# One core, attention, experts and a dense pair: the numerator of a rational function nested from PSUM, tokens scaled by a diagonal product, and eight pieces of w_out made float32 earlier

## The chip, the cores and the metric

The kernel runs on one core of one Trainium2 chip. The metric is the device time of one execution in microseconds (us), the median of several runs. The engines go by the names of the profile: PE is the matrix engine (PEld its weight loads), DVE the vector engine, ACT the scalar engine, POOL the GpSimd engine and SP the queue that starts most DMAs. L12 is line 12 of the kernel before, unless the text says that it is of the changed kernel.

## The reference

Three stages follow each other. The third is the one that most of this is about.

```python
x = attention(q_l, k_l, v_l, q_g, k_g, v_g)     # 2304 tokens of 512
e = argmax(x @ w_gate)                          # one of 8 experts for each token
y = c * (relu(x @ w1[e]) @ w2[e])               # c: one factor for each token
h = y @ w_in                                    # 512 -> 2048
P = a[0] + a[1]*h + a[2]*h**2 + a[3]*h**3
Q = 1.0 + abs(b[0])*abs(h) + abs(b[1])*h**2
out = (P / (Q + 1e-6)) @ w_out                  # 2048 -> 512
```

[...] For precision every product runs on numbers that are split into two parts of a reduced float32 (high and low), and three of the four part products are summed.

## The kernel before

**Attention** (up to some 160 us into the span) ends with the gate of the last batch, a chain of small operations written as a generator that is advanced a few steps at a time between the matmuls of expert 0. Its last part writes the lists of tokens: L624 on DVE, a transpose on PE (L627) and a copy on DVE (L629).

**The experts** follow one another, 0 to 7. The tokens of an expert are gathered by an indirect DMA of POOL in blocks of 128 (L755), multiplied by their factor c (`scale`: L767 on ACT or L769 on POOL or DVE, 128x512), transposed by four PE instructions against an identity (`prep`, L780) and split (L760 on ACT, L761 on DVE). `wide` then runs eight pieces of 12 matmuls into a `ph` tile (L870; two such tiles), with relu and split on ACT and DVE (L875, L876), and two pieces later 12 matmuls into `acc` (L882). Between them, in 32 slots for one expert, a plan hands out other work by a letter: `s` splits a piece of the next expert's weights (L682 on ACT, then L686 on POOL or DVE), `c` is one of three DVE operations that make a piece of `w_in` or `w_out` float32 (`conv_step`: L703, L706, L709, all into the one tile `f`), `g` gathers, `x` scales and `p` transposes. After the third operation SP writes the piece to DRAM (L727) and loads the next 64-bit piece (L729), so the next L703 waits for that write. SP also loads the next expert's weights (L672), in the same order as the program.

**The dense pair** (`moe2`, from 458 us) takes the tokens in five chunks of 4, 3, 4, 3 and 3 tiles of 128 (`CH`). A chunk has 16 steps, one for each 128 columns of h: PE computes h two steps ahead (L1090, 12 matmuls of 512 or 384 columns) and multiplies by a piece of `w_out` three steps behind (L1138, 12 or 9 matmuls of 512). Between the two lies the rational function of one step, over three engines:

- ACT: sq = h*h (L1099), q = |b0 h| (L1100), u = a3 h + a2 (L1102);
- DVE: q = b1 sq + q (L1101). POOL: u = u sq (L1103);
- of the step before, the split of the quotient: gh on ACT (L1108), gl on POOL in the first 16 steps and on DVE after (L1109);
- ACT: r0 = exp(-ln(q + 1 + 1e-6)) in two instructions (L1111, L1112);
- DVE: u = a1 h + u (L1116), then a step of Newton (L1119, L1122) and u = (u + a0) r (L1126).

Through the first 16 steps (chunk 0) `w_out` is made ready, a piece a step, by a generator that is advanced once after each of L1116, L1119 and L1122: three DVE operations make a piece float32 (L703, L706, L709 again, into `io`), then ACT and POOL split it (L1170, L1171). Two of the sixteen pieces come as float32 from DRAM, since they were made during the experts (`NPRE`); for them those three advances do nothing. Where the next chunk's tokens are split (L1045 on ACT, L1046 on DVE), a step has two more operations. At the end of a chunk the results are copied out of PSUM (L1147) and scattered by POOL (L1149, L1150). Each engine works through its instructions in program order.

Of the kernel before, what the change touches and what calls it, by code (L numbers as in the profile page):

```python
# [42 lines left out]
NX = 4  # L43
SA, S0, S1 = "v", "a", "p"

# [9 lines left out]

NPRE, NCONV = 2, 9
WLO = lambda nc, f: nc.gpsimd
PLANW = plan(32, s=range(0, 31, 2), c=range(2, 29, 3), g=(6, 9, 20, 24), x=(1, 2, 16, 18), p=(5, 8, 19, 22))
PLANW7 = plan(32, s=range(2, 18, 2))
# [23 lines left out]
AHEAD = 2  # L83
GL = lambda nc, s: nc.gpsimd if GL0 <= s < 16 else nc.vector
GL0 = 0
CH = (4, 3, 4, 3, 3)
ER = {"sq": 1, "q": 2, "u": 2, "r0": 1}
CQ = lambda nc: nc.sync
# [13 lines left out]
class Build:  # L102
# [26 lines left out]
    def attn_consts(self, ap, inner):  # L129
# [362 lines left out]
    def gate(self, b, xT=None, woven=0):  # L492
# [126 lines left out]
        if last:  # L619
            self.places(self.idx, self.tab)  # L620
            self.counts()
            yield

            nc.vector.tensor_tensor(out=self.wrap, in0=self.tab, in1=self.wrap, op=ALU.subtract)  # L624
            yield
            pt = ps_m.tile([128, 512], F32, tag="xps", name="lgT")[:, 0:128]
            nc.tensor.transpose(pt, self.wrap[:, 0:128], self.ident)  # L627
            yield
            nc.vector.tensor_copy(self.idxT, pt)  # L629
        elif b == B - 2:  # L630
# [25 lines left out]
    def load_raw(self, e, pc):  # L656

        nc, t = self.nc, self.t
        if e > 9 or pc >= (16 - NPRE // 2 if e == 9 else 8):
            return  # L660
        r = self.raws[e, pc] = self.raw[pc % 4]
        if e == 9 and pc >= NPRE // 2:
            RQ(nc).dma_start(out=r.bitcast(I64), in_=t["w64"][16 + NPRE // 2 + pc])
            return
        if e < E:
            if pc < 4:
                src = t["w1"][e][:, pc, :].rearrange("p (a f) -> p a f", a=2)
            else:
                src = t["w2"][e][:, 2 * pc - 8:2 * pc - 6, :]
        else:  # L670
            src = self.wf[16 * (e - 8) + 2 * pc:16 * (e - 8) + 2 * pc + 2].rearrange("a p f -> p a f")
        RQ(nc).dma_start(out=r.rearrange("p (a f) -> p a f", a=2), in_=src)  # L672
# [47 lines left out]
    def conv_step(self, k):  # L720

        q, n = divmod(k, 3)
        if not 0 <= q < 16 + NPRE:
            return
        self.conv_op(self.r64[q % 2], self.f32[q % NF], n)
        if n == 2:
            CQ(self.nc).dma_start(out=self.wf[q], in_=self.f32[q % NF].bitcast(F32))  # L727
            if q + 2 < 16 + NPRE:
                CQ(self.nc).dma_start(out=self.r64[q % 2], in_=self.t["w64"][q + 2])  # L729

# [52 lines left out]

    def experts(self, st, first, gate):
# [184 lines left out]
        def woven():  # L969
# [87 lines left out]
    def moe2(self):  # L1057
        nc, tc, out = self.nc, self.tc, self.t["out"]
        with ExitStack() as st:
# [257 lines left out]
```

## Time and profile before

| | before |
|---|---|
| median of 3 runs | 904.21 us (902.74 to 906.9) |
| the profiled execution | 907.55 us, its span 905.9 us |
| busy in the span | PE 812.4 us (90%), DVE 681.7 (75%), ACT 520.9 (58%), POOL 411.4 (45%) |
| the chain that ended last | DVE 31% of the span, ACT 9%, issue 6%, POOL 2%, PE 1% |

A busy PE is not a PE at its peak. In the timelines a line has the start in us from the span's start, the busy time in us, the engine, the line and operation, and output and inputs; what ended an idle time stands in brackets.

### The profile page before, as it was taken

How to read it: one execution, taken by the hardware profiler on the slowest of the kernel's cores; microseconds unless marked ns; L12 is line 12 of the kernel's file. 1: busy time of each engine (PE TensorE's matmuls, PEld its weight loads, DVE VectorE, ACT ScalarE, POOL GpSimd, SP SyncE). 2: the span in 40 equal slices, each digit the busy share in tenths (PEclk: the TensorE clock that was granted, in tenths of full speed). 3: DMA queues.
4: the chain of work that ended last, by engine and by line, in shares of the span. 5: the costliest groups of instructions: out<-in, count | busy, mean ns of one | idle time of the engine just before them, and what ended most of it. 6: DMA issues, size and time to landing. Idle time of an engine off the chain costs nothing. (4 is left out here: it accounts for less than half of the span.)

```text
span 905.9 us, 17033 instructions
## 1 busy us (share of the span) xinstructions
PE 812.4 (90%) x6093; PEld 675.6 (75%) x6093; DVE 681.7 (75%) x1428; ACT 520.9 (58%) x1195; POOL 411.4 (45%) x443
## 2 busy tenths in 40 slices
PE   7999998888998998899996987789999998998994
PEld 4767765776988898887974755577778887987882
DVE  4678777752836775661479999989989997998895
ACT  3667666343544554442465555567776766777664
POOL 3445546452747776650465555542242234223322
PEclk8999999998999999999997999999999999999998
DMA  8798872561738788760433223011000001000000
GB/s 289 238 318 267 271 248 77 161 223 46 262 118 284 258 275 274 237 227 26 154 118 93 82 70 94 1 46 36 13 35 12 13 1 47 1 1 12 24 1 36
DMA packets 48626, 112.94 MB, mean 125 GB/s; under 512 B 8763, under 2 KB 20204, under 8 KB 46466
## 3 DMA queue, kind: packets, MB, share of 16 engines
q1 hardware_dynamic: 39938, 97.18, 33.1%
q0 software_dynamic: 4288, 10.06, 3.6%
q10 hardware_dynamic: 4288, 4.29, 1.5%
q8 instruction: 59, 0.97, 0.5%
q14 instruction: 53, 0.43, 0.1%
HBM read 96.47 MB, written 18.98 MB: 127 GB/s over the span
## 5 line engine op out<-in xcount | busy, mean ns | idle before, releaser
L1103 POOL TENSOR_TENSOR u<-u,sq 128x384 f32<-128x384 f32 (+1 forms) x80 | 104.4, 1305 | 201.0 <-ACT u L1102 198.8
L1138 PE MATMUL acc<-slot,gh 128*128 128x512 f32 x544 | 175.9, 402 | 14.9 <-ACT raw L1147 5.6
L1090 PE MATMUL ph<-x2c,slot 128*128 128x512 f32 (+1 forms) x576 | 136.0, 387 | 15.8 <-DVE u L1116 13.7
L686 POOL TENSOR_TENSOR slot<-raw,slot 128x512 fp32r<-128x512 f32 x80 | 111.5, 1398 | 69.5 <-ACT slot L682 64.1
L1090 PEld LDWEIGHTS ph<-x2c,slot 128*128 128x128 f32 x576 | 107.1, 192 | 40.5 <-DVE u L1116 19.1
L1138 PEld LDWEIGHTS acc<-slot,gh 128*128 128x128 f32 x544 | 102.6, 191 | 41.7 <-POOL slot L1171 7.5
L1138 PE MATMUL acc<-slot,gl 128*128 128x512 f32 x272 | 109.0, 401 | 1.0 <-DVE gl L1109 1.0
L882 PE MATMUL acc<-hT,slot 128*128 128x256 f32 (+1 forms) x768 | 105.1, 288 | 0.2 <-DVE hT L876 0.2
L882 PEld LDWEIGHTS acc<-hT,slot 128*128 128x128 f32 x768 | 98.4, 192 | 0.4 <-DVE hT L876 0.4
L1101 DVE SCALAR_TENSOR_TENSOR q<-sq,cab,q 128x384 f32<-128x384 f32 (+1 forms) x80 | 95.9, 1199 | 2.2 <-ACT q L1100 1.8
L682 ACT CAST slot<-raw 128x512 fp32r<-128x512 f32 x144 | 84.1, 618 | 13.6 <-DVE yt L888 5.6
L1108 ACT CAST gh<-u 128x384 fp32r<-128x384 f32 (+1 forms) x80 | 44.6, 558 | 78.4 <-DVE u L1126 57.1
L1090 PE MATMUL ph<-xa,slot 128*128 128x384 f32 x384 | 75.8, 346 | 10.7 <-DVE u L1116 10.7
L1090 PEld LDWEIGHTS ph<-xa,slot 128*128 128x128 f32 x384 | 68.3, 192 | 18.9 <-DVE u L1116 17.4
L1111 ACT ACTIVATE r<-q,cab 128x384 f32<-128x384 f32 (+1 forms) x80 | 52.9, 661 | 50.3 <-DVE q L1101 49.7
L312 POOL TENSOR_SCALAR pr<-ex,r 128x128 f32<-128x128 f32 x128 | 46.6, 376 | 67.4 <-PE sc L258 20.8
L686 DVE TENSOR_TENSOR slot<-raw,slot 128x512 fp32r<-128x512 f32 x64 | 60.8, 953 | 10.1 <-ACT slot L682 8.7
L1122 DVE SCALAR_TENSOR_TENSOR r<-q,r 128x384 f32<-128x384 f32 (+1 forms) x80 | 64.9, 811 | 2.3
L1126 DVE SCALAR_TENSOR_TENSOR u<-u,cab,r 128x384 f32<-128x384 f32 (+1 forms) x80 | 64.3, 803 | 2.3
L1116 DVE SCALAR_TENSOR_TENSOR u<-ph,cab,u 128x384 f32<-128x384 f32 (+1 forms) x80 | 52.8, 660 | 13.2 <-POOL u L1103 13.2
L1138 PEld LDWEIGHTS acc<-slot,gl 128*128 128x128 f32 x272 | 51.5, 189 | 14.7 <-DVE gl L1109 2.6
L294 ACT ACTIVATE ex<-sm,mx 128x128 f32<-128x128 f32 x128 | 50.2, 395 | 16.8 <-POOL pr L312 8.5
(202 smaller groups left out, 1548.4 us busy)
## 6 DMA issues: line engine op xcount, KB each, us to landing
raw<-in_w_dram SPq DMA_DIRECT2D x78, 512.0 KB
vw<-in_vw_dram SPq DMA_DIRECT2D x16, 1024.0 KB
r<-in_w_dram SPq DMA_DIRECT2D x18, 512.0 KB
kw<-in_kw_dram SPq DMA_DIRECT2D x16, 384.0 KB
wf<-f SPq DMA_DIRECT2D x18, 256.0 KB
raw<-wf SPq DMA_DIRECT2D x9, 512.0 KB
qt<-in_qT_dram SPq DMA_DIRECT2D x32, 128.0 KB
xbuf<-xrow SPq DMA_DIRECT2D x8, 512.0 KB
```

The source lines that it names most:

```text
L294: nc.scalar.activation(ex[:, h], src[:, h], AF.Exp, bias=mx[:, h:h + 1], scale=-1.0, accum_out=ssum[:, h:h + 1])
L682: nc.scalar.copy(hi, r)
L686: eng.tensor_tensor(out=lo[:, c], in0=r[:, c], in1=hi[:, c].bitcast(F32), op=ALU.subtract)
L882: nc.tensor.matmul(acc[m][:, :n], lhsT=W[:, b, 8 + f, 128 * m:128 * m + 128], rhs=hT[f % nh][:, a, :n], start=(f == 0 and i == 0), stop=(f ...
L1090: nc.tensor.matmul(ph[:, :w], lhsT=l[a], rhs=r[b], start=(k == 0 and i == 0), stop=(k == 3 and i == 2))
L1101: nc.vector.scalar_tensor_tensor(out=q, in0=sq, scalar=b1, in1=q, op0=ALU.mult, op1=ALU.add)
L1103: nc.gpsimd.tensor_tensor(out=u, in0=u, in1=sq, op=ALU.mult)
L1111: nc.scalar.activation(r0, q, AF.Ln, bias=eps1)
L1116: nc.vector.scalar_tensor_tensor(out=u, in0=h, scalar=a1, in1=u, op0=ALU.mult, op1=ALU.add)
L1122: nc.vector.scalar_tensor_tensor(out=r0, in0=q, scalar=2.0, in1=r0, op0=ALU.subtract, op1=ALU.mult, reverse0=True)
L1126: nc.vector.scalar_tensor_tensor(out=u, in0=u, scalar=a0, in1=r0, op0=ALU.add, op1=ALU.mult)
L1138: nc.tensor.matmul(accs[i], lhsT=l[a], rhs=Wo[:, b, f, :], start=(f == 0 and j == 0), stop=(f == 15 and j == 2))
```

## The change

Four things are changed.

1. **Numerator and denominator of the rational function.** ACT computes ab = |h|, u = a3 h + a2 and q = b1 ab + b0, the last from SBUF. POOL computes q = q ab. DVE computes u = h u and u = (u + a1) h, both with h read from PSUM. gl is on DVE in all steps. The number of instructions of ACT in a step stays at six, that of DVE is six in every step, that of POOL one.
2. **Tokens are scaled by a diagonal.** `scale` writes c times the identity (128x128) into `dg`, by ACT where POOL did it; `prep` multiplies the raw tokens by it on PE in place of the transpose.
3. **Pieces of w_out.** Every other piece, eight in place of two, is made float32 during the experts: 12 operations an expert in place of 9. In `w_out` a piece of 64 bits and one of float32 alternate.
4. **The last lists** of the gate move into a generator that is advanced between the matmuls of expert 0; the copy goes to ACT.

```diff
-SA, S0, S1 = "v", "a", "p"
+SA, S0, S1 = "v", "a", "a"
-NPRE, NCONV = 2, 9
+NPRE, NCONV = 8, 12
+LOADS = [l for j in range(NPRE // 2) for l in ((4 * j, 4 * j + 2), (4 * j + 1,), (4 * j + 3,))]
-PLANW = plan(32, s=range(0, 31, 2), c=range(2, 29, 3), g=(6, 9, 20, 24), x=(1, 2, 16, 18), p=(5, 8, 19, 22))
+PLANW = plan(32, s=range(0, 31, 2), c=(2, 3, 7, 8, 12, 13, 17, 18, 21, 23, 25, 27), g=(6, 9, 20, 24), x=(1, 2, 16, 18), p=(5, 8, 19, 22))
-GL = lambda nc, s: nc.gpsimd if GL0 <= s < 16 else nc.vector
+GL = lambda nc, s: nc.vector
-            yield
-            nc.vector.tensor_tensor(out=self.wrap, in0=self.tab, in1=self.wrap, op=ALU.subtract)
-            yield
-            pt = ps_m.tile([128, 512], F32, tag="xps", name="lgT")[:, 0:128]
-            nc.tensor.transpose(pt, self.wrap[:, 0:128], self.ident)
-            yield
-            nc.vector.tensor_copy(self.idxT, pt)
+    def lists(self):
+        self.nc.vector.tensor_tensor(out=self.wrap, in0=self.tab, in1=self.wrap, op=ALU.subtract)
+        yield
+        yield
+        pt = self.ps_m.tile([128, 512], F32, tag="xps", name="lgT")[:, 0:128]
+        self.nc.tensor.transpose(pt, self.wrap[:, 0:128], self.ident)
+        yield
+        self.nc.scalar.copy(self.idxT, pt)
...
-        xg = self.xgs[j % len(self.xgs)][:rows]
-        x, c = xg[:, :DM], xg[:, DM:]
+        d, c = self.dg[j % len(self.dg)][:rows, :rows], self.xgs[j % len(self.xgs)][:rows, DM:]
         if eng == "a":
-            self.nc.scalar.activation(x, x, AF.Copy, scale=c)
+            self.nc.scalar.activation(d, self.ident[:rows, :rows], AF.Copy, scale=c)
...
-            nc.tensor.transpose(pt[:, c], xg[:rows, 128 * c:128 * c + 128], self.ident[:rows, :rows])
+            nc.tensor.matmul(pt[:, c], lhsT=xg[:rows, 128 * c:128 * c + 128], rhs=self.dg[j % len(self.dg)][:rows, :rows],
+                             start=True, stop=True)
...
+        self.dg = [r[:, 0:128] for r in hr]
...
-                    nc.scalar.activation(sq, h, AF.Square)
-                    nc.scalar.activation(q, h, AF.Abs, scale=b0)
-                    nc.vector.scalar_tensor_tensor(out=q, in0=sq, scalar=b1, in1=q, op0=ALU.mult, op1=ALU.add)
+                    nc.scalar.activation(ab, h, AF.Abs)
                     nc.scalar.activation(u, h, AF.Identity, scale=a3, bias=a2)
-                    nc.gpsimd.tensor_tensor(out=u, in0=u, in1=sq, op=ALU.mult)
+                    nc.scalar.activation(q, ab, AF.Identity, scale=b1, bias=b0)
+                    nc.gpsimd.tensor_tensor(out=q, in0=q, in1=ab, op=ALU.mult)
+                    nc.vector.tensor_tensor(out=u, in0=h, in1=u, op=ALU.mult)
+                    nc.vector.scalar_tensor_tensor(out=u, in0=u, scalar=a1, in1=h, op0=ALU.add, op1=ALU.mult)
+                    for _ in range(SPN(s)[0]):
+                        next(sp, None)
...
-                    nc.vector.scalar_tensor_tensor(out=u, in0=h, scalar=a1, in1=u, op0=ALU.mult, op1=ALU.add)
-                    for _ in range(SPN(s)[0]):
-                        next(sp, None)
                     nc.vector.scalar_tensor_tensor(out=q, in0=q, scalar=1.0 + 1e-6, in1=r0, op0=ALU.add, op1=ALU.mult)
```

Three places show how the order of the instructions moves.

DVE in chunk 0 of the dense pair, before: one step, with a piece of `w_out` being made float32 (`io`).

```order
L1101 SCALAR_TENSOR_TENSOR q_8580<-sq_8578,cab,q_8580 128x512
L1116 SCALAR_TENSOR_TENSOR u_8582<-ph_8913,cab,u_8582 128x512
L709 SCALAR_TENSOR_TENSOR io<-raw_77,io 128x512
L1119 SCALAR_TENSOR_TENSOR q_8580<-q_8580,r_8583 128x512
L703 TENSOR_SCALAR io<-raw_74 128x512
L1122 SCALAR_TENSOR_TENSOR r_8583<-q_8580,r_8583 128x512
L706 SCALAR_TENSOR_TENSOR io<-raw_74,io 128x512
L1126 SCALAR_TENSOR_TENSOR u_8582<-u_8582,cab,r_8583 128x512
```

And in the change: a step that ends a piece (L714 of the changed kernel is its third operation) and the next, which has none of the three until its L1128.

```order
L1112 TENSOR_TENSOR u_8613<-ph_8984,u_8613 128x512
L1113 SCALAR_TENSOR_TENSOR u_8613<-u_8613,cab,ph_8984 128x512
L714 SCALAR_TENSOR_TENSOR io<-raw_77,io 128x512
L1121 TENSOR_TENSOR gl_8607<-u_8614,gh_8604 128x512
L1128 SCALAR_TENSOR_TENSOR q_8611<-q_8611,r_8615 128x512
L1131 SCALAR_TENSOR_TENSOR r_8615<-q_8611,r_8615 128x512
L1135 SCALAR_TENSOR_TENSOR u_8613<-u_8613,cab,r_8615 128x512
L1200 SCALAR_TENSOR_TENSOR od_8617<-order,od_8617 128x17
L1112 TENSOR_TENSOR u_8614<-ph_9027,u_8614 128x512
L1113 SCALAR_TENSOR_TENSOR u_8614<-u_8614,cab,ph_9027 128x512
L1121 TENSOR_TENSOR gl_8608<-u_8613,gh_8605 128x512
L1128 SCALAR_TENSOR_TENSOR q_8612<-q_8612,r_8615 128x512
```

L1101 is gone, L1112 and L1113 stand where L1101 and L1116 stood, gl (L1121) has come to DVE, and the two conversions between L1128 and L1135 stand in every second step only.

ACT in a step of 512 columns after chunk 0 (chunk 2), before:

```order
L1099 ACTIVATE sq_8578<-ph_10205 128x512
L1100 ACTIVATE q_8580<-ph_10205,cab 128x512
L1102 ACTIVATE u_8582<-ph_10205,cab 128x512
L1108 CAST gh_8573<-u_8581 128x512
L1111 ACTIVATE r_8583<-q_8580,cab 128x512
L1112 ACTIVATE r_8583<-r_8583 128x512
```

And in the change:

```order
L1108 ACTIVATE ab_8610<-ph_10210 128x512
L1109 ACTIVATE u_8614<-ph_10210,cab 128x512
L1110 ACTIVATE q_8612<-ab_8610,cab 128x512
L1120 CAST gh_8605<-u_8613 128x512
L1123 ACTIVATE r_8615<-q_8612,cab 128x512
L1124 ACTIVATE r_8615<-r_8615 128x512
```

The last of the three ACT operations ahead of gh now makes q, which goes through POOL before the logarithm (L1123 of the changed kernel) can start.

DVE in an even expert, before:

```order
L876 SCALAR_TENSOR_TENSOR hT_3362<-ph,hT_3362 128x256
L686 TENSOR_TENSOR slot_3337<-raw_74,slot_3337 128x512
L703 TENSOR_SCALAR f_0_3786<-r_1_3785 128x512
L876 SCALAR_TENSOR_TENSOR hT_3363<-ph,hT_3363 128x256
L706 SCALAR_TENSOR_TENSOR f_0_3786<-r_1_3785,f_0_3786 128x512
L761 TENSOR_TENSOR xa<-pt,xa 128x4x128
L686 TENSOR_TENSOR slot_3337<-raw_75,slot_3337 128x512
L876 SCALAR_TENSOR_TENSOR hT_3364<-ph,hT_3364 128x256
```

And in the change:

```order
L884 SCALAR_TENSOR_TENSOR hT_3364<-ph,hT_3364 128x256
L691 TENSOR_TENSOR slot_3339<-raw_74,slot_3339 128x512
L708 TENSOR_SCALAR f_0_3788<-r_0_3786 128x512
L711 SCALAR_TENSOR_TENSOR f_0_3788<-r_0_3786,f_0_3788 128x512
L884 SCALAR_TENSOR_TENSOR hT_3365<-ph,hT_3365 128x256
L767 TENSOR_TENSOR xa<-pt,xa 128x4x128
L691 TENSOR_TENSOR slot_3339<-raw_75,slot_3339 128x512
L714 SCALAR_TENSOR_TENSOR f_0_3788<-r_0_3786,f_0_3788 128x512
L884 SCALAR_TENSOR_TENSOR hT_3366<-ph,hT_3366 128x256
L708 TENSOR_SCALAR f_0_3788<-r_1_3787 128x512
L767 TENSOR_TENSOR xa<-pt,xa 128x4x128
```

The first operation on the next piece (L708) follows the third on the piece before (L714) with one L884 between them, where a wait for the write of `f` can now stand; two more operations on pieces of w_out lie among the expert's own.

## Rows read from the trace of the kernel before

**Rows 1.** Windows: us, busy us of each engine, clock, DMA share; experts, then chunk 0.

```profile
285.70:401.30 115.60, 102.56 (x834) 100.79 (x834) 78.21 (x124) 57.60 (x120) 81.19 (x64) 0.97 0.79 259
458.00:586.00 128.00, 103.01 (x426) 79.32 (x424) 124.55 (x141) 75.57 (x125) 69.23 (x51) 0.96 0.25 76
```

**Rows 2.** Chain that ended last: start us, us, what; chunk 0, then chunk 3.

```profile
547.09 1.70 DVE r L1122
577.74 1.68 DVE r L1122
773.58 1.39 DVE q L1101
831.74 1.38 DVE q L1101
```

**Rows 3.** Timeline of PE (start us, us, engine line op, tiles); four tiles, then three.

```profile
719.58 2.96 PE L1090 MATMUL ph<-x2c,slot 128*128 128x512 f32 x12
725.17 2.96 PE L1090 MATMUL ph<-x2c,slot 128*128 128x512 f32 x12
735.66 2.26 PE L1090 MATMUL ph<-xa,slot 128*128 128x384 f32 x12
737.76 0.63 PE L1138 MATMUL acc<-slot,gh 128*128 128x512 f32 x2
```

**Rows 4.** Timeline of DVE and POOL in chunk 0, steps of 512 columns.

```profile
478.32 0.68 DVE L1122 SCALAR_TENSOR_TENSOR r<-q,r 128x512 f32<-128x512 f32 x1
478.57 1.58 POOL L1103 TENSOR_TENSOR u<-u,sq 128x512 f32<-128x512 f32 x1 [0.45 <-ACT u L1102]
478.93 1.77 DVE L706 SCALAR_TENSOR_TENSOR io<-raw,io 128x512 int32<-128x512 int32 x1
481.95 0.74 DVE L1116 SCALAR_TENSOR_TENSOR u<-ph,cab,u 128x512 f32<-128x512 f32 x1
482.09 1.27 POOL L1109 TENSOR_TENSOR gl<-u,gh 128x512 fp32r<-128x512 f32 x1 [1.94 <-ACT gh L1108]
```

**Rows 5.** Timeline of one step of chunk 3, 384 columns, ACT, DVE and POOL.

```profile
811.48 0.62 ACT L1111 ACTIVATE r<-q,cab 128x384 f32<-128x384 f32 x1 [0.72 <-DVE q L1101]
812.13 0.53 ACT L1112 ACTIVATE r<-r 128x384 f32<-128x384 f32 x1
812.56 0.47 ACT L1099 ACTIVATE sq<-ph 128x384 f32<-128x384 f32 x1
813.39 0.67 ACT L1102 ACTIVATE u<-ph,cab 128x384 f32<-128x384 f32 x1
813.87 0.62 DVE L1126 SCALAR_TENSOR_TENSOR u<-u,cab,r 128x384 f32<-128x384 f32 x1
814.14 1.22 POOL L1103 TENSOR_TENSOR u<-u,sq 128x384 f32<-128x384 f32 x1 [3.11 <-ACT u L1102]
815.81 0.62 ACT L1111 ACTIVATE r<-q,cab 128x384 f32<-128x384 f32 x1 [0.72 <-DVE q L1101]
```

**Rows 6.** Timeline of DVE where chunk 1 begins, in brackets its idle time and releaser.

```profile
601.37 0.62 DVE L1116 SCALAR_TENSOR_TENSOR u<-ph,cab,u 128x384 f32<-128x384 f32 x1 [2.74 <-POOL u L1103]
```

**Rows 7.** Groups by line: tiles, shapes, count | busy us, mean ns | idle and releasers.

```profile
L780 PE MATMUL pt<-ident,xg 128*128 128x128 f32 (+1 forms) x132 | 20.8, 284 | 14.2 <-POOL xg L769 10.1 <-DVE xa L761 3.4 <-PE sc L258 0.6
L627 PE MATMUL lgT<-ident,wrap 128*128 128x128 f32 x1 | 0.5, 475 | 2.4 <-DVE wrap L624 2.4
L258 PE MATMUL sc<-kw,qt 128*64 128x128 f32 x512 | 47.6, 308 | 1.6 <-DVE mx L264 0.8 <-DMA kw<-in_kw_dram 0.8
```

**Rows 8.** Timeline of SP and DVE in an expert, then groups by line.

```profile
354.39 0.33 SPq L727 DMA_DIRECT2D wf<-f  x1
358.48 0.43 DVE L703 TENSOR_SCALAR f<-r 128x512 int32<-128x512 int32 x1 [2.41 <-DMA wf<-f]
...
L703 DVE TENSOR_SCALAR f<-r 128x512 int32<-128x512 int32 x18 | 11.6, 643 | 16.7 <-DMA wf<-f 10.7 <-issue 4.9 <-DVE x2c L761 1.0
L882 PE MATMUL acc<-hT,slot 128*128 128x256 f32 (+1 forms) x768 | 105.1, 288 | 0.2 <-DVE hT L876 0.2
```

More of the change, by code (lines that the diff above doesn't have):

```diff
@@ L83 @@
 AHEAD = 2
-GL = lambda nc, s: nc.gpsimd if GL0 <= s < 16 else nc.vector
-GL0 = 0
+GL = lambda nc, s: nc.vector
 CH = (4, 3, 4, 3, 3)
-ER = {"sq": 1, "q": 2, "u": 2, "r0": 1}
+ER = {"ab": 1, "q": 2, "u": 2, "r0": 1}
 CQ = lambda nc: nc.sync
@@ L142, in attn_consts @@
         self.wg, self.tok = wg.rearrange("p (c e) -> p c e", c=4), tok
+        self.dg = [ap.tile([128, 128], F32, name=f"dg{n}") for n in range(2)]
         self.xTg = inner.tile([128, NP, 128], F32, name="xTg")
@@ L658, in load_raw @@
         nc, t = self.nc, self.t
-        if e > 9 or pc >= (16 - NPRE // 2 if e == 9 else 8):
+        if e > 9 or pc >= (len(LOADS) if e == 9 else 8):
             return
         r = self.raws[e, pc] = self.raw[pc % 4]
-        if e == 9 and pc >= NPRE // 2:
-            RQ(nc).dma_start(out=r.bitcast(I64), in_=t["w64"][16 + NPRE // 2 + pc])
+        if e == 9 and len(LOADS[pc]) == 1:
+            RQ(nc).dma_start(out=r.bitcast(I64), in_=t["w64"][16 + LOADS[pc][0]])
             return
@@ L670, in load_raw @@
         else:
-            src = self.wf[16 * (e - 8) + 2 * pc:16 * (e - 8) + 2 * pc + 2].rearrange("a p f -> p a f")
+            q = 2 * pc if e == 8 else 16 + LOADS[pc][0] // 2
+            src = self.wf[q:q + 2].rearrange("a p f -> p a f")
         RQ(nc).dma_start(out=r.rearrange("p (a f) -> p a f", a=2), in_=src)
@@ L728, in conv_step @@
             if q + 2 < 16 + NPRE:
-                CQ(self.nc).dma_start(out=self.r64[q % 2], in_=self.t["w64"][q + 2])
+                n = q + 2 if q < 14 else 16 + 2 * (q - 14)
+                CQ(self.nc).dma_start(out=self.r64[q % 2], in_=self.t["w64"][n])
     def counts(self):
@@ L761, in split_t, with scale @@
         self.nc.vector.tensor_tensor(out=lo, in0=pt, in1=hi.bitcast(F32), op=ALU.subtract)
-    def scale(self, j, rows=128, eng="p"):
-        xg = self.xgs[j % len(self.xgs)][:rows]
-        x, c = xg[:, :DM], xg[:, DM:]
+    def scale(self, j, rows=128, eng="a"):
+        d, c = self.dg[j % len(self.dg)][:rows, :rows], self.xgs[j % len(self.xgs)][:rows, DM:]
         if eng == "a":
-            self.nc.scalar.activation(x, x, AF.Copy, scale=c)
+            self.nc.scalar.activation(d, self.ident[:rows, :rows], AF.Copy, scale=c)
         else:
             (self.nc.gpsimd if eng == "p" else self.nc.vector).tensor_scalar(
-                out=x, in0=x, scalar1=c, scalar2=1.0, op0=ALU.mult, op1=ALU.mult)
+                out=d, in0=self.ident[:rows, :rows], scalar1=c, scalar2=1.0, op0=ALU.mult, op1=ALU.mult)
     def prep(self, j, x, ps, at=None, rows=128, scale=True, skip=0):
@@ L983, in woven @@
                 pass
-            yield from todo(0, PLAN0, 1, blocks(1, (0, 1)) + blocks(0, (2, 3)),
-                            blocks(1, (0, 1)) + blocks(0, (2, 3)) + blocks(2, (0, 1)) + blocks(1, (2, 3)))
+            yield from weave(todo(0, PLAN0, 1, blocks(1, (0, 1)) + blocks(0, (2, 3)),
+                                  blocks(1, (0, 1)) + blocks(0, (2, 3)) + blocks(2, (0, 1)) + blocks(1, (2, 3))),
+                             self.lists())
         acc = [ps_a.tile([128, 512], F32, tag=f"acc{m}", name=f"acc{m}") for m in range(4)]
@@ L1097, in elem @@
                     h = hs.pop(s)[:, :w]
-                    sq, q, u, r0 = (et[t_][s % len(et[t_])][:, :w] for t_ in ("sq", "q", "u", "r0"))
-                    nc.scalar.activation(sq, h, AF.Square)
-                    nc.scalar.activation(q, h, AF.Abs, scale=b0)
-                    nc.vector.scalar_tensor_tensor(out=q, in0=sq, scalar=b1, in1=q, op0=ALU.mult, op1=ALU.add)
+                    ab, q, u, r0 = (et[t_][s % len(et[t_])][:, :w] for t_ in ("ab", "q", "u", "r0"))
+                    nc.scalar.activation(ab, h, AF.Abs)
                     nc.scalar.activation(u, h, AF.Identity, scale=a3, bias=a2)
-                    nc.gpsimd.tensor_tensor(out=u, in0=u, in1=sq, op=ALU.mult)
+                    nc.scalar.activation(q, ab, AF.Identity, scale=b1, bias=b0)
[4 more added lines that the diff above has]
+                        next(sp, None)
                 if 1 <= s <= n_steps:
@@ L1158, in w_out @@
             def w_out():
+                where = {f: (pc, i) for pc, l in enumerate(LOADS) for i, f in enumerate(l)}
+                done, nxt = set(), 4
                 for f in range(16):
-                    pc = f // 2 if f < NPRE else f - NPRE // 2
-                    if f < NPRE:
-                        w = self.raws[9, pc][:, 512 * (f % 2):512 * (f % 2) + 512]
+                    pc, i = where[f]
+                    if len(LOADS[pc]) == 2:
+                        w = self.raws[9, pc][:, 512 * i:512 * i + 512]
                         for k in range(3):
@@ L1171, in w_out @@
                     WLO(nc, f).tensor_tensor(out=Wo[:, 1, f, :], in0=w, in1=Wo[:, 0, f, :].bitcast(F32), op=ALU.subtract)
-                    if f >= NPRE or f % 2:
-                        self.load_raw(9, pc + 4)
+                    done.add(f)
+                    while nxt < len(LOADS) and done.issuperset(LOADS[nxt - 4]):
+                        self.load_raw(9, nxt)
+                        nxt += 1
             sp = w_out()
```

## The prediction, as put on record before the change ran

> **What bounds the kernel now.** I read the windows first, to see which engine is full in which stage, then the chain that ended last for the pace of a step, then timelines for single steps, and last the groups by line and their waits for the experts. In chunk 0 of the dense pair DVE is busy for 124.55 of 128.00 us and PE for 103.01 [rows 1]: DVE sets the pace there. Four steps lie between the two L1122 of the chain, (577.74 - 547.09) / 4 = 7.66 us a step [rows 2]. PE alone would need 5.59 us for the 24 matmuls of such a step (725.17 - 719.58) [rows 3], that is 0.233 each. After chunk 0 there is no conversion of `w_out`, and the two meet. A step of 512 columns runs at PE's 5.59. A step of 384 columns needs 2.10 us for L1090 (737.76 - 735.66) and 9 x 0.233 = 2.10 for L1138, 4.20 in all [rows 3], and takes 4.33 from one logarithm to the next (815.81 - 811.48) [rows 5]; 13 steps of chunk 3, three or four of them with a split of the next tokens, average (831.74 - 773.58) / 13 = 4.47 [rows 2]. Here the loop of ACT and DVE sets the pace, 0.13 to 0.27 behind PE. In the experts PE is busy for 102.56 of 115.60 us, DVE for 78.21, and DMA for 0.79 [rows 1]: PE is the bound, with holes.
>
> **What two engines do to each other.** L1122 took 0.68 us with POOL free; L706, of the same size and kind, took 1.77 when a POOL operation had started 0.36 before it [rows 4]: 1.09 lost to one meeting. L1116, which reads h from PSUM, took 0.74 with POOL's L1109 in the middle of it [rows 4]. The other way round, L1126 had started first, kept its 0.62, and POOL's L1103 ended 0.87 after it [rows 5]. So a DVE operation on SBUF alone and a POOL operation exclude each other, first come first, and one with PSUM on one side is free. The changed numerator has both its operations on PSUM.
>
> **The step of 384 columns, walked.** E is the end of Exp, 812.66. ACT starts its next operation 0.10 before E, the next after 0.37, and the third 0.56 after that, which is u's 0.67 less the same overlap [rows 5]. So ab starts at -0.10, u at 0.27 and q at 0.83. q reads SBUF with two scalars, which no row shows; between Exp's 0.53 and u's 0.67 I take 0.65. POOL's product is ready at about 1.55. DVE's last operation holds from 1.21 to 1.83 as before, so the product ends at 1.83 + 0.87 = 2.70. The two new DVE operations (0.6 each, as L1116 has 0.62 at this size [rows 6]) lie beside it. The logarithm starts 0.08 later, Exp 0.65 after that, and E comes again at 2.70 + 0.08 + 0.65 + 0.53 = 3.96. That is under PE's 4.20, so PE takes over: 13 steps in each of chunks 1 and 3 go from 4.47 to 4.25 (splits do not all hide), and 13 in chunk 4 from 4.33 to 4.20. That makes -5.7 and -1.7, **-7.5**. Its ends are -9.5 (4.20 everywhere) and +8 (4.53, if the loop is 0.57 longer than walked). Steps of 512 columns after chunk 0 are PE's before and after: 0.
>
> **Chunk 0.** A step that converts loses one of three meetings with POOL (-1.09) and gets gl back (+0.68, as L1122): -0.41. Against that the logarithm now waits for POOL, which also has the split of `w_out`; I give the 0.41 back and take 0 for these eight. Six further steps lose their conversion: 0.43 (L703 [rows 8]) and twice 0.68, 1.79 us, of which 0.5 is spent on waiting for the product. I take -1.3 x 6 = **-8**. The other two had none before. Ends: all fourteen at PE's pace, 14 x (5.59 - 7.66) = -29; or nothing, 0.
>
> **Boundaries and ends.** Where chunk 1 begins, DVE waited 2.74 us for POOL's product behind the scatters [rows 6], with the logarithm long done. Now the logarithm and Exp, 1.18 us, come after that product, where L1116's 0.62 [rows 6] came: +0.56 at four boundaries, **+2.2**. Filling the pipe and draining it are each about one us longer by ACT's third operation and POOL's: **+2**. Ends 0 and +8 for both.
>
> **Tokens.** PE sat idle for 10.1 us in front of transposes because POOL's scaling was late [rows 7]; it stands in POOL's queue between splits of weights. A diagonal of 128 columns on ACT costs less than the 0.53 of an Exp of 384 [rows 5], and nothing on POOL. ACT now waits for gathers itself, with L875 behind it, and `dg` shares its memory with `hr`, so once or twice it waits for a store. I take **-8**; ends -10 and 0. The product itself: a plain float32 matmul of 128 columns has a mean of 308 ns, the transpose 284 [rows 7]. Over 132 that is 3 us at the most; the longer one reads its weights with a stride, so I take 0. The Trainium skill, FP8 and Floating Point Precision, TensorE Precision Notes, says that true float32 takes four passes through the array. By that four times a quarter of 0.233 would be paid for each, an estimate of up to 23 us more in the sum; the 308 beside the 284 speaks against it, and it is the fourth rival below.
>
> **The lists.** PE waited 2.4 us for L624 [rows 7]; now matmuls of expert 0 stand there: **-2**, ends -2.4 and 0.
>
> **More conversion in the experts.** Eighteen DVE operations, 6 x 1.79 = 11 us, lie on an engine with 37 us free in 115 [rows 1]. Six writes and six 64-bit loads join SP's queue, in front of weight loads that are four pieces ahead; DMA has a fifth of its time left; in chunk 0 SP has 12 loads of `w_out` in place of 15. The new wait: L703 waits for the write of `f`, which was issued at 354.39 and let L703 start at 358.48, 4.1 us [rows 8]. With two pairs of pieces an expert now back to back, DVE stands still up to 12 x 4.1 = 49 us, and L876 and the splits queue behind it. Before, such waits made 10.7 us and PE waited for L876 for 0.2 [rows 8]: two tiles of `ph` cover a late L876. I take **+2**; ends 0 and +18 (a third of the 49 uncovered).
>
> **Sum.** -7.5 - 8 + 2.2 + 2 - 8 - 2 + 2 = -19.3. The profiled execution took 907.55, 3.3 above the median of the runs, and would take 888.3; from the median 904.21 it is 884.9. I predict **885 us**.
>
> **Rivals.**
> - *Chunk 0 falls further.* With POOL down to two operations a step, DVE may win the meetings, and converting steps go from 7.66 to 6.5, the others from 6.36 to PE's 5.6. For: only luck of order holds the 0.41 back. Against: both POOL operations start while DVE has SBUF work. 885 - 8 x 1.16 - 8 x 0.76 = 870.
> - *The stalls in the experts show.* For: two waits of 4 us an expert are new; against: the 0.2 above. It decides when DVE is later than the two `ph` tiles cover. 885 - 2 + 18 = 901.
> - *Slower: the new operations on h exclude POOL after all.* Then the product gets its turn only at 3.03, after both, ends at 3.90, and E comes again at 5.16 in place of 4.33 over some 42 steps: 885 + 7.5 + 35 = 927. It decides when the product ends later than 3.07 after E. For: they read SBUF too. Against: L1116 and L1109 above.
> - *The diagonal product is a full float32 one.* Place: PE in the experts, the bound there. If it takes 128 columns as long as L1090 takes 512, 0.233, and not the quarter of it, 0.058, it adds 132 x 0.175 = 23: 885 + 23 = 908. For: it has no row of its own. Against: 308 beside 284. This is also what the page named above would make of it.
> - *It does not do what it says:* float32 pieces come late from DRAM, the chunk waits for its loads as long as it converted. For: loads now wait for two pieces to be done; against: two steps of lead. The 8 of chunk 0 are lost and a step of 7.66 while the first wait fills: 885 + 16 = 901.
>
> **How the numbers follow.** My forecast (876 to 897) 0.54, the five rivals 0.17, 0.13, 0.07, 0.04 and 0.05. A change of 0.5%, 4.5 us, is about what a measurement can tell from none: faster is below 899.7, slower above 908.7. Faster: 0.54 + 0.17 + 0.02 of the second rival, 0.73. Slower: 0.07 and 0.02 from the tops of the second and fourth, 0.09. The same: 0.18. The range, 866 to 904, takes in the first, second and fifth rival and leaves out the third and part of the fourth.
>
> **What would show it.** Right: DVE busy falls in chunk 0 and steps alternate at about 7.7 and 6.3; steps of 384 columns at 4.2 with PE full; no PE wait for scaling. Wrong: the two operations on h at over 1 us beside POOL; the logarithm waiting for POOL for over 1 us a step; PE waiting for L876 in the experts; the diagonal product well above 0.3 us.

## The result and the profile after

The changed kernel takes **916.81 us** (median of 4 runs, 914.43 to 919.59) against 904.89 for the kernel before in the same session: a ratio of 1.013, 95% interval 1.0097 to 1.0164. It is slower by more than the half per cent that a measurement can tell. The forecast was 885, its range 866 to 904. The profiled execution has a span of 914.7 us, 8.8 more than before.

Three events cut the span: the first copy of expert 0's result by ACT, PE's first matmul of h, and the logarithms (there are 80, one a step).

| stage, us | before | after | change |
|---|---|---|---|
| start to the end of expert 0 | 198.90 | 197.06 | -1.84 |
| experts 1 to 7 | 255.51 | 290.16 | **+34.65** |
| first h to first logarithm | 6.82 | 8.20 | +1.38 |
| chunk 0 (logarithms 1 to 17) | 120.89 | 112.03 | **-8.86** |
| chunks 1 to 4 (17 to 80) | 309.86 | 293.63 | **-16.23** |
| last logarithm to the end | 13.92 | 13.59 | -0.33 |

So the dense pair gave 24 us, twice what I had worked out, and the experts took 35 away. The windows of after show both; the first is the stretch of four experts that [rows 1] has at 115.60 us, the second chunk 0, the third chunks 1 to 4. Columns: the stretch and its length in us; busy us (instructions) of PE, PEld, DVE, ACT, POOL; granted clock of TensorE (1.00 is its upper level, 0.50 its lower); DMA share; GB/s.

```profile
299.58:432.67 133.09, 114.44 (x898) 111.28 (x897) 81.69 (x139) 62.94 (x137) 57.55 (x46) 0.94 0.76 250
495.42:607.45 112.03, 94.55 (x394) 73.45 (x392) 108.97 (x130) 70.76 (x117) 47.20 (x32) 0.95 0.20 63
607.45:901.08 293.63, 284.42 (x1339) 243.22 (x1340) 233.68 (x394) 221.29 (x401) 98.15 (x93) 1.00 0.05 19
```

In the experts PE has 64 instructions more than in [rows 1] (898 and 834), is busy for 12 us more and idle for 5.6 more (18.65 of 133.09 against 13.04 of 115.60). Both need a cause. The groups by line of the experts (197 to 487 us) name two:

```profile
L890 PE MATMUL acc<-hT,slot 128*128 128x256 f32 (+1 forms) x681 | 94.7, 289 | 19.0 <-DVE hT L884 19.0
L786 PE MATMUL pt<-hr,xg 128*128 128x128 f32 x208 | 29.7, 288 | 5.2 <-issue 4.2 <-ACT hr L773 1.0
L708 DVE TENSOR_SCALAR f<-r 128x512 int32<-128x512 int32 x24 | 14.1, 588 | 44.0 <-DMA wf<-f 28.2 <-issue 15.9
```

First, L708 (L703 before) stood for 44.0 us where it had stood for 16.7 [rows 8], and PE's second product L890 (L882 before) waited 19.0 for `hT` of L884 (L876 before), where it had waited 0.2. Second, the diagonal product L786 has **208 records for 104 products** (26 blocks of four), and L780 had one record for each transpose [rows 7]. (A record is one instruction as the profile lists it; "issue" is idle time for which the profile names no releaser.) The timelines show how the first comes about. SP in an expert:

```profile
410.61 0.33 SPq L677 DMA_DIRECT2D raw<-in_w_dram  x1
411.18 1.19 SPq L732 DMA_DIRECT2D wf<-f  x1
```

DVE in the same stretch (idle time and releaser in brackets):

```profile
410.46 0.68 DVE L714 SCALAR_TENSOR_TENSOR f<-r,f 128x512 int32<-128x512 int32 x1
411.07 0.42 DVE L884 SCALAR_TENSOR_TENSOR hT<-ph,hT 128x256 fp32r<-128x256 f32 x1
415.16 1.12 DVE L708 TENSOR_SCALAR f<-r 128x512 int32<-128x512 int32 x1 [3.68 <-DMA wf<-f]
416.21 0.68 DVE L767 TENSOR_TENSOR xa<-pt,xa 128x512 fp32r<-128x512 f32 x1
...
429.95 0.43 DVE L708 TENSOR_SCALAR f<-r 128x512 int32<-128x512 int32 x1 [0.74 <-DMA wf<-f]
430.29 0.42 DVE L884 SCALAR_TENSOR_TENSOR hT<-ph,hT 128x256 fp32r<-128x256 f32 x1
```

The write issued at 411.18 frees `f` at 415.16, 4.0 us later, as the 4.1 of [rows 8]; DVE does nothing meanwhile. At 429.95 the last piece of the expert begins late, the `hT` behind it on DVE is late too, and PE waits for it:

```profile
424.75 2.62 PE L890 MATMUL acc<-hT,slot 128*128 128x256 f32 x19
430.77 2.08 PE L890 MATMUL acc<-hT,slot 128*128 128x256 f32 x8 [3.40 <-DVE hT L884]
```

(424.75 + 2.62 to 430.77: 3.40 idle.) TensorE's granted clock, 1.00 until then, fell to its lower level in this wait. The first window below is PE's idle time up to the fall, the second the 6.8 us from it on:

```profile
427.37:429.70 2.33, 0.00 (x0) 0.00 (x0) 1.84 (x2) 0.00 (x0) 0.70 (x1) 1.00 0.31 113
429.70:436.50 6.80, 5.73 (x25) 5.54 (x26) 4.23 (x9) 1.75 (x4) 0.00 (x0) 0.50 0.70 220
```

Five of the six waits of this kind have such a stretch that begins within 1.6 us of their end. In experts 1 to 7 the clock is at its lower level for 34 us in all.

A stretch of chunk 3, steps of 384 columns, answers to [rows 5]; ACT:

```profile
822.05 0.53 ACT L1124 ACTIVATE r<-r 128x384 f32<-128x384 f32 x1
822.48 0.47 ACT L1108 ACTIVATE ab<-ph 128x384 f32<-128x384 f32 x1
822.85 0.67 ACT L1109 ACTIVATE u<-ph,cab 128x384 f32<-128x384 f32 x1
823.41 0.70 ACT L1110 ACTIVATE q<-ab,cab 128x384 f32<-128x384 f32 x1
825.40 0.62 ACT L1123 ACTIVATE r<-q,cab 128x384 f32<-128x384 f32 x1 [0.31 <-POOL q L1111]
826.05 0.53 ACT L1124 ACTIVATE r<-r 128x384 f32<-128x384 f32 x1
```

POOL and then DVE, one step earlier:

```profile
820.19 1.18 POOL L1111 TENSOR_TENSOR q<-q,ab 128x384 f32<-128x384 f32 x1 [2.82 <-ACT q L1110]
...
820.41 0.55 DVE L1112 TENSOR_TENSOR u<-ph,u 128x384 f32<-128x384 f32 x1
821.00 0.61 DVE L1113 SCALAR_TENSOR_TENSOR u<-u,cab,ph 128x384 f32<-128x384 f32 x1
```

From Exp to Exp it is 4.00 us; I had walked 3.96. The two new operations on h ran at 0.55 and 0.61 beside POOL's product, the first of them wholly inside it, so they do not exclude it. PE in the same stretch takes 4.19 us from one step's first matmul of h to the next, with no idle time between:

```profile
818.48 2.26 PE L1099 MATMUL ph<-xa,slot 128*128 128x384 f32 x12
822.67 1.56 PE L1099 MATMUL ph<-x2c,slot 128*128 128x384 f32 x8
```

### The profile page after: what moved, and what is told of

Same layout as the page of the kernel before. It is cut to its first block, busy times and chain, and to the rows that moved or that the text cites. A ratio compares the mean times of both kernels' runs of the same rounds, so it can differ in the third digit from the quotient of the medians.

```text
span 914.7 us, 17332 instructions
## 1 busy us (share of the span) xinstructions
PE 826.4 (90%) x6225; PEld 694.3 (76%) x6225; DVE 628.3 (69%) x1443; ACT 536.4 (59%) x1222; POOL 353.2 (39%) x401
## 5 line engine op out<-in xcount | busy, mean ns | idle before, releaser
L1147 PE MATMUL acc<-slot,gh 128*128 128x512 f32 x544 | 172.5, 396 | 7.8 <-ACT gh L1120 3.3
L1111 POOL TENSOR_TENSOR q<-q,ab 128x384 f32<-128x384 f32 (+1 forms) x80 | 103.8, 1298 | 190.2 <-ACT q L1110 185.5
L691 POOL TENSOR_TENSOR slot<-raw,slot 128x512 fp32r<-128x512 f32 x80 | 105.9, 1327 | 130.2 <-ACT slot L687 125.0
L890 PE MATMUL acc<-hT,slot 128*128 128x256 f32 (+1 forms) x768 | 108.2, 291 | 19.0 <-DVE hT L884 19.0
L890 PEld LDWEIGHTS acc<-hT,slot 128*128 128x128 f32 x768 | 99.2, 193 | 20.8 <-DVE hT L884 20.2
L1128 DVE SCALAR_TENSOR_TENSOR q<-q,r 128x384 f32<-128x384 f32 (+1 forms) x80 | 50.0, 625 | 54.4 <-ACT r L1124 52.8
L1099 PE MATMUL ph<-xa,slot 128*128 128x384 f32 x384 | 73.5, 339 | 7.1 <-DVE u L1113 7.1
L1123 ACT ACTIVATE r<-q,cab 128x384 f32<-128x384 f32 (+1 forms) x80 | 52.7, 659 | 40.9 <-POOL q L1111 40.9
L1135 DVE SCALAR_TENSOR_TENSOR u<-u,cab,r 128x384 f32<-128x384 f32 (+1 forms) x80 | 65.7, 821 | 2.6
L691 DVE TENSOR_TENSOR slot<-raw,slot 128x512 fp32r<-128x512 f32 x64 | 54.6, 856 | 10.4 <-ACT slot L687 9.3
L878 PE MATMUL ph<-xa,slot 128*128 128x256 f32 x384 | 56.8, 303 | 5.1 <-PEq L970 3.2
L1131 DVE SCALAR_TENSOR_TENSOR r<-q,r 128x384 f32<-128x384 f32 (+1 forms) x80 | 58.4, 730 | 2.5
L1110 ACT ACTIVATE q<-ab,cab 128x384 f32<-128x384 f32 (+1 forms) x80 | 59.7, 747 | 0.0
```

The lines of the kernel that those rows point to most:

```text
L691: eng.tensor_tensor(out=lo[:, c], in0=r[:, c], in1=hi[:, c].bitcast(F32), op=ALU.subtract)
L878: nc.tensor.matmul(ph, lhsT=W[:, b, 2 * k + s // 4, c:c + 128], rhs=x[:, a, k, :n], start=(i == 0), stop=(i == 11))
L890: nc.tensor.matmul(acc[m][:, :n], lhsT=W[:, b, 8 + f, 128 * m:128 * m + 128], rhs=hT[f % nh][:, a, :n], start=(f == 0 and i == 0), stop=(f ...
L1099: nc.tensor.matmul(ph[:, :w], lhsT=l[a], rhs=r[b], start=(k == 0 and i == 0), stop=(k == 3 and i == 2))
L1110: nc.scalar.activation(q, ab, AF.Identity, scale=b1, bias=b0)
L1111: nc.gpsimd.tensor_tensor(out=q, in0=q, in1=ab, op=ALU.mult)
```

## The experiments

Two theories stood at first. **W**: the waits for the write of `f` hold DVE, and PE behind it. **D**: the diagonal product takes PE twice as many instructions, and that is the loss. All ratios are to the kernel before, measured in the same session, with 95% intervals.

**1. A second buffer for the pieces.** The idle half of `hr` becomes the second `f`; both diagonals move into the other half. Work and DMAs are the same.

```diff
-NF = 1
+NF = 2
...
-        self.dg = [r[:, 0:128] for r in hr]
+        self.dg = [hr[0][:, 128 * n:128 * n + 128] for n in range(2)]
...
+        self.f32.append(hr[1].bitcast(I32))
```

> The changed kernel with a second buffer for the float32 pieces (the idle half of the memory of `hr`), so that a piece need not wait until the piece before it is written to DRAM. Theory W (the waits for the write of `f` hold DVE, `hT` stands behind them, and PE waits): the 28.2 us of L708 behind wf<-f go to under 5, PE's wait for L884 goes from 19.0 to under 6, the experts take some 15 to 20 us less: 897 to 902 us. Theory D (the experts are longer because the diagonal product is issued in two passes): 913 to 918, whatever the waits do. A third case: the wait moves on to the 64-bit load (two buffers), which then ends as late: 908 to 914.

Measured 888.58 us, ratio 0.9807 (0.9744 to 0.987): 28 us less than the changed kernel. W holds, by more than I expected (897 to 902). The groups by line: no wait on L708 is left, those for loads included, and none of PE on `hT`. The clock is at its lower level for 17 us of the experts, where it was for 34: the experts gave back 25.1 us, more than the 19.0 that PE had waited for `hT`.

```profile
L890 PE MATMUL acc<-hT,slot 128*128 128x256 f32 (+1 forms) x768 | 104.7, 287 | 0.0
L708 DVE TENSOR_SCALAR hr<-r 128x512 int32<-128x512 int32 x12 | 9.8, 813 | 0.0
L708 DVE TENSOR_SCALAR f<-r 128x512 int32<-128x512 int32 x12 | 9.7, 806 | 0.0
```

**2. The same work at other places, one buffer.** In the changed kernel the third operation of a piece and the first of the next are 1, 4, 2 and 7 places apart (7 to 8, 13 to 17, 21 to 23, 27 to 2 of the next expert); before they were 3, 3 and 8. Here they are 6 everywhere. Of the line of `PLANW` only its `c` is shown.

```diff
-c=(2, 3, 7, 8, 12, 13, 17, 18, 21, 23, 25, 27)
+c=(2, 3, 4, 10, 11, 12, 18, 19, 20, 26, 27, 28)
```

> The changed kernel, one buffer, its twelve operations an expert at other places: three in a row, then six places free, so that no piece begins less than 6 places (some 6 us) after the piece before it was written. Work, writes and loads are the same. If distance in the plan is what decides: the 28.2 us of L708 behind wf<-f go to under 6 and PE's 19.0 behind L884 to under 4: 888 to 895. If it's the amount of conversion or DMA in the experts: 912 to 918.

Measured 896.9, ratio 0.99 (0.9865 to 0.9934), 20 less than the changed kernel and a little above the expected band. L708's waits are gone here as well:

```profile
L708 DVE TENSOR_SCALAR f<-r 128x512 int32<-128x512 int32 x24 | 12.4, 517 | 0.9 <-DMA wf<-f 0.9
```

So it was distance, not the amount of conversion. That it stays 8 behind the second buffer isn't explained by these waits. In the profiles the experts differ by 5.6 us (270.69 and 265.07), and PE's waits at the branches between experts by 4.7 of it (9.6 and 4.9); experiment 9 has the two plans 2 us apart, so the 8 may be scatter.

**3. The old plan of conversion** in the changed kernel: two pieces of `w_out` early, nine operations an expert. One line that numbers the pieces is left out, and of `PLANW` only its `c` is shown.

```diff
-NPRE, NCONV = 8, 12
+NPRE, NCONV = 2, 9
-LOADS = [l for j in range(NPRE // 2) for l in ((4 * j, 4 * j + 2), (4 * j + 1,), (4 * j + 3,))]
+LOADS = [(0, 1)] + [(f,) for f in range(2, 16)]
...
-c=(2, 3, 7, 8, 12, 13, 17, 18, 21, 23, 25, 27)
+c=range(2, 29, 3)
```

> The changed kernel with the old plan of conversion: two pieces of w_out and not eight, nine operations an expert, every third place. Theory W: PE's wait for L884 falls from 19.0 to under 2 and the experts give back some 20 us, chunk 0 takes 5 to 8 more for the six pieces that it converts again: 902 to 907. Theory D: the experts stay, chunk 0 takes 8 more: 922 to 926.

Measured 902.45, ratio 0.9946 (0.9915 to 0.9978). Experts 1 to 7 take 268.84 us (290.16 in the changed kernel), chunk 0 121.06 (112.03): 21 come back, 9 are paid, as W said, and PE no longer waits for `hT` (0.0). But the experts are still 13 over those of before, with the waits of before (10.1 for the write of `f`). That much is not W.

**4. The old scaling and transposes** in the changed kernel.

```diff
-SA, S0, S1 = "v", "a", "a"
+SA, S0, S1 = "v", "a", "p"
...
-            nc.tensor.matmul(pt[:, c], lhsT=xg[:rows, 128 * c:128 * c + 128], rhs=self.dg[j % len(self.dg)][:rows, :rows],
-                             start=True, stop=True)
+            nc.tensor.transpose(pt[:, c], xg[:rows, 128 * c:128 * c + 128], self.ident[:rows, :rows])
```

(and `scale` in place on the tokens, on POOL, as in the kernel before.)

> The changed kernel with tokens scaled in place on POOL and transposed, as before the change. Theory W: 132 passes on PE less, 0.43 us a block times 33 = 14 us, against 10 us of waiting for POOL that come back, and PE partly waits for DVE anyhow: 908 to 916. Theory D: most of the 33 us of the experts go away: 885 to 895.

Measured 906.56, ratio 0.9991 (0.9953 to 1.0029): 10 less, just under W's band and far from D's. The product costs something, though with the waits in place DVE holds PE anyway (PE waited 22.5 us for `hT`), so its full price can't be read here.

**5. The numerator alone**, on the kernel before (point 1 of the change, gl on DVE with it, nothing else).

> The kernel before with the new numerator alone (and all of gl on DVE). If the numerator by itself is what made the dense pair 24 us shorter (451.5 to 427.5): 880 to 888. If the conversion that left chunk 0 made 8 of it: 887 to 892. If the numerator gives no more than the 11 us that I worked out less the 8 of chunk 0: 900 to 905.

Measured 888.07, ratio 0.9797 (0.9732 to 0.9861). Chunk 0 takes 121.07 us (120.89 before), chunks 1 to 4 292.81 (309.86). The numerator gives **17 us after chunk 0 and nothing in it**; the 9 of chunk 0 are the conversion's.

**6. Numerator and lists**, with the conversion, scaling and transposes of before: what is left of the change when points 2 and 3 are undone.

> The kernel before with the new numerator and the lists moved, nothing else. Numerator alone: 888.1. If the lists bring the 2.4 us that PE waited for them: 885 to 887; if that wait was covered elsewhere: 888. Against the run with nine operations an expert and the diagonal (902.5) it shows what the diagonal product costs by itself: 14 to 18 if it is two passes, under 4 if it costs what a transpose costs.

Measured 886.4, ratio 0.9796 (0.9744 to 0.9849): the lists give 1.7 in the medians, within their scatter. Against experiment 3 it isolates point 2 of the change, the diagonal product and its scaling on ACT: 16 us in the medians, 14 by the two ratios. Windows over experts 1 to 7, experiment 3 and then this:

```profile
197.42:466.26 268.84, 245.43 (x1802) 231.10 (x1800) 135.74 (x227) 120.72 (x264) 104.75 (x81) 0.96 0.57 188
```

```profile
196.10:447.65 251.55, 229.58 (x1698) 214.68 (x1696) 141.94 (x227) 112.86 (x238) 136.09 (x107) 0.98 0.62 202
```

104 records more on PE and 15.85 us more busy, of 17.29 that the stage is longer. Not all of it is the product's: the granted clock is 0.96 in the first and 0.98 in the second. The timeline of PE has the price of one block. In this run a block of transposes lets the next work start after 0.36 us (317.60 - 317.24), in experiment 3 a block of products after 0.81 (333.02 - 332.21):

```profile
317.24 0.60 PE L786 MATMUL pt<-ident,xg 128*128 128x128 f32 x4
317.60 1.62 PE L876 MATMUL ph<-x2c,slot 128*128 128x256 f32 x12
```

```profile
332.21 1.05 PE L786 MATMUL pt<-hr,xg 128*128 128x128 f32 x8
333.02 0.95 PE L890 MATMUL acc<-hT,slot 128*128 128x256 f32 x6
```

0.45 us a block, times 33, is 15 us. Of the 33 blocks 26 lie in these windows, 12 us; the other 4 of the 15.85 go with the lower clock.

**7. Both repaired**: experiment 1 (second buffer) with experiment 4.

> Both parts that seem to cost undone: a second buffer for the pieces, and tokens scaled on POOL and transposed as before the change. If the price of the diagonal product (902.5 with nine operations an expert against 888.1 of the numerator alone, the lists 2: 16 us) and that of the waits (916.8 against 888.6: 28) add up: 872 to 876. If they hide each other, as the 10 us of the kernel with the waits and the transposes say: 878 to 884.

Measured 884.81, ratio 0.9762 (0.9718 to 0.9807). That is just above the second band. The two prices do not add up here: only 4 us below experiment 1. PE waits 8.4 us for POOL's scaling, and the granted clock of the last five experts is 0.96.

**8. The same, scaled by ACT in place** (`S1 = "a"`, 128x512).

> The same with the tokens scaled in place by ACT, 128x512, 0.72 us each where the diagonal took 0.40. If what PE waited for was POOL's queue, these waits (9.8 us in the kernel with the numerator alone) go: 5 to 9 under the kernel that scales on POOL. If ACT is as late (PE waited 5.5 for the diagonal): the same within 3 us.

Measured **877.94**, ratio 0.9696 (0.9662 to 0.973), 7 under experiment 7 and 10.6 under experiment 1. PE's wait for scaling is 3.8 us, though ACT's operation is longer than the diagonal was:

```profile
L773 ACT ACTIVATE xg<-xg 128x512 f32<-128x512 f32 x30 | 21.7, 724 | 0.8 <-DMA xg<-xbuf,idx 0.5 <-ACTq L1010 0.3
L786 PE MATMUL pt<-ident,xg 128*128 128x128 f32 (+1 forms) x132 | 20.7, 281 | 5.7 <-ACT xg L773 3.8 <-DVE xa L766 0.8 <-issue 0.6
```

**9. Its variants**, on one chip: with nine operations an expert and one buffer; with one buffer and the places of experiment 2; with all sixteen pieces made in the experts (`NPRE, NCONV = 16, 18`); and the kernel itself again.

> Nine operations an expert as before the change, tokens scaled in place by ACT and transposed. The same with POOL's scaling took 886.4. If ACT's scaling frees what PE waited for POOL (9.0 us): 877 to 881. If moving six pieces out of chunk 0 is worth its 9 us only when the experts hide it (second buffer): this is some 2 to 5 us behind the kernel with second buffer and ACT's scaling (877.9).

> One buffer, twelve operations an expert at the wider distances, transposes and ACT's scaling in place. If the price of the diagonal product is PE's own (14 us), it comes off the 896.9 of the wider distances in full: 881 to 885. If PE was held by something else there: 890 or more.

> All sixteen pieces of w_out made float32 in the experts (eighteen operations an expert), second buffer, ACT's scaling, transposes. If the experts hide it and the eight steps of chunk 0 that still convert gain as the six did (9 us): 867 to 872. If DVE (112.6 of 166 us busy in the last five experts) or the DMA queues (0.70) become the bound in the experts: 878 to 890.

> The kernel with second buffer and ACT's scaling once more, on the same chip as its three variants: 873 to 880.

Measured 880.17, 879.14, 881.59 and 877.03, ratios 0.9722 (0.9681 to 0.9762), 0.9713 (0.967 to 0.9756), 0.9736 (0.9689 to 0.9782) and 0.968 (0.9636 to 0.9724): the intervals overlap, all four beat both kernels, and none is shown to be better than the others. The first and the last came as expected. The second is 18 us under experiment 2, a little more than the price of the product; its expectation said 12 to 16. So moving the six pieces, at its best, is worth some 3 us in the medians, which is not shown to differ from nothing. The third fell in its second band. With all sixteen, chunk 0 falls to 102.84 us, but the experts rise to 269.09, and the waits return in another form, for the loads of the 64-bit pieces:

```profile
L888 PE MATMUL acc<-hT,slot 128*128 128x256 f32 (+1 forms) x768 | 109.4, 293 | 18.1 <-DVE hT L882 18.1
L707 DVE TENSOR_SCALAR f<-r 128x512 int32<-128x512 int32 x16 | 17.2, 1076 | 10.6 <-DMA r<-in_w_dram 9.1 <-DVEq L968 1.0 <-DVEq L970 0.5
```

The stages of the profiled executions side by side:

| us | experts 1 to 7 | chunk 0 | chunks 1 to 4 |
|---|---|---|---|
| before | 255.51 | 120.89 | 309.86 |
| the change | 290.16 | 112.03 | 293.63 |
| 1 second buffer | 265.07 | 112.04 | 293.31 |
| 2 other places | 270.69 | 112.06 | 293.58 |
| 3 old conversion | 268.84 | 121.06 | 292.79 |
| 4 old transposes | 284.06 | 112.39 | 293.47 |
| 5 numerator alone | 251.53 | 121.07 | 292.81 |
| 6 numerator, lists | 251.55 | 121.05 | 292.76 |
| 7 buffer, transposes, POOL | 262.74 | 112.03 | 292.77 |
| 8 buffer, transposes, ACT | 251.08, again 255.70 | 112.03 | 293.28, 293.33 |
| 9 nine operations, one buffer | 248.42 | 121.10 | 293.56 |
| 9 other places, one buffer | 256.24 | 112.01 | 293.39 |
| 9 all sixteen pieces | 269.09 | 102.84 | 292.50 |

The dense pair repeats to a few tenths of a us, the experts to about 4: experiments 5 and 6 have the experts of before in 251.5, where before took 255.5, and experiment 8 shows both values. The clock goes with it: PE's work of this stage, the same in both, is busy for 231.46 us before, at a granted clock of 0.97, and for 227.79 in experiment 5, at 0.99. Prices in the experts are good to some 4 us.

## Why the prediction was wrong

**More conversion in the experts, "I take +2; ends 0 and +18": failed.** It measured +21 (290.16 - 268.84, experiment 3); the waits alone, with all the conversion kept, were worth 25 (290.16 - 265.07, experiment 1). The mechanism was in the text, the wait for the write and what is queued behind it; I had DVE standing for up to 49 us, and it stood for 44. What failed is the cover: "two tiles of `ph` cover a late L876". They cover it inside an expert, where PE's first product (L878) waited for them 1.1 us in all. At its end no further `ph` follows, and a late `hT` is a late end: six waits, one at the end of each of experts 1 to 6, 19.0 us in all, the longest 3.7. Against experiment 1, PE in the experts is idle for 15.5 us more (290.16 - 253.11 against 265.07 - 243.53) and, with the same instructions, busy for 9.6 more, at a granted clock of 0.94 for 0.97. The second rival was the right one, and its 18 was too small: it had the waits, and not the lower clock beside them.

**The diagonal product, "so I take 0": failed.** I set the 308 ns of L258 beside the 284 of a transpose. But [rows 7] has L258 with 512 records, and the program has 256 of these products: a float32 product of this kind, whose numbers are not split as those of the experts and the dense pair are, is two records, and the row is the mean of a half. Nor is a record's mean what it holds PE up by, since records overlap. Per product the next work starts 0.20 us later (0.81 / 4), per transpose 0.09 (0.36 / 4): by records the two are alike, and what doubled is their number. This makes 15 us by the timeline, 14 to 16 by experiments 3 and 6. The sign that I had named for it, "well above 0.3 us", could not show it: the row has 288 ns a record. No run shows a price of the stride that I gave as the reason for 0. The fourth rival, 23 us, had the right mechanism; I gave it 0.04. The Trainium skill, FP8 and Floating Point Precision, TensorE Precision Notes, gives true float32 four passes through the array. The trace shows two records for a product, not four; but its 0.20 us is 3.5 times the quarter of 0.233 that I set for a pass, so in time the rule was nearer than my row.

**Tokens, -8: came in part.** The idle time in front of these blocks fell from 14.2 us before to 7.6 in the changed kernel, and from 11.4 in experiment 6 to 8.1 in experiment 3. The seven waits for POOL's scaling, 10.1, are gone by name, but the longest, 3.2 at the end of expert 0, stayed as one of 3.2 under "issue". PE's waits at the branches between experts were 11.3 in experiment 3 and 6.0 in experiment 6, but 3.9 in the changed kernel itself: they are no price of the diagonal. Experiment 8, ACT scaling in place with the transposes kept, has the short waits without the product.

**Chunk 0, -8: right in the sum**, -8.9. The converting steps were worth 0, as taken (121.07 with the numerator alone), and the six lost conversions give 9.0. It stays DVE's: 108.97 of 112.03 us. The steps are not those that I described: they do not alternate at 7.7 and 6.3, but come at 6.6 to 7.3 from the third on, two together at 14 as forecast. That the gains and losses inside a converting step cancel was chosen, not worked out, and no run takes them apart.

**Steps of 384 columns -7.5, of 512 columns 0, boundaries +2.2: right in the walk of a step, wrong in the sum**, -5.3 against -16.2. Chunks 1 to 4 gave 2.8, 5.3, 4.3 and 3.9 us; chunk 2 is the one of 512 columns, for which I had 0. The walk of a step was right, 4.00 for 3.96, and PE does take over at 4.20. I took PE's pace for the steps in the middle of a chunk and charged the boundaries apart. But a loop that is faster than PE (4.00 for 4.20, and 4.89 between logarithms for 5.59 at 512 columns) catches up after a boundary instead of falling behind again. By an estimate from these two paces PE alone needs 47 x 4.20 + 16 x 5.59 = 286.8 us from logarithm 17 to 80; before took 23.0 more, now it is 6.8 more. "512 columns: 0" and "boundaries +2.2" are the terms that failed. The ends were wrong too: by the paces given, 4.20 everywhere is -8.7 and not -9.5 (26 x 0.27 + 13 x 0.13), and +8 counts all 39 steps from 4.33, though 26 of them were set at 4.47.

**Filling and draining +2, lists -2:** +1.05 and -1.84. **The first rival** (chunk 0 falls by 15 more), **the third** (the operations on h exclude POOL) and **the fifth** (late pieces of `w_out`) did not happen.

The whole, stage by stage in the profiles: dense pair -24.0, lists -1.8, diagonal product and scaling +17.3 (experiment 3 less 6), conversion +21.3 (the change less experiment 3), less the 4.0 by which the experts of before happened to be longer than those of experiment 6. That is the +8.8 of the profile; since each step starts where the one before it ended, the sum must close and is no check. The failed terms lie on both sides: without the 11 us that chunks 1 to 4 gave beyond the forecast the change would have been slower still.

## What to carry to other kernels

Before a duration from a row is used as the price of an instruction, compare the row's count with the number of such instructions in the program: a mean over halves is not the price of the whole. Operations that an in-order engine runs for later belong at least as far behind the start of the write that frees their buffer as that write takes (here some 4 us), or they need a second buffer; what hides a late operation in the middle of a stage does not hide it at the end. And price a pipelined stretch from its total against the bounding engine's own need, since a loop that is made faster than that engine also gives back its stalls at boundaries.

## What was not expected of the hardware

A float32 product of 128 columns left two records on PE and took 0.20 us to the transpose's 0.09. Five of six waits of PE of some 3 us stood beside stretches at the lower clock, and with the waits gone (experiment 1) PE was not only less idle, by 15.5 us, but busy for 9.6 us less with the same instructions. Open are the 7 us between scaling by POOL and by ACT (experiments 7 and 8), of which PE's waits for scaling make 4.6 (8.4 and 3.8), and why the branches between experts took 11.3 us of PE in one run, 6.0 in another and 3.9 in the changed kernel.
